# A transformer block with modulated LayerNorm: another order of normalising, transposing and modulating ahead of attention

## The chip, the cores and the metric

The kernel runs on one core of a Trainium2 chip (trn2). The metric is device time in microseconds (us); lower is better. The core has five engines with instruction streams of their own: TensorE (PE), VectorE (DVE), ScalarE (ACT), GpSimd (POOL) and SyncE (SP), which here issues all DMA transfers.

## The reference

The input has 2048 tokens of 1024 features; all tensors are bf16. There are 32 query heads of 32 features, one key head and one value head shared by all queries, and a feed-forward part with 3584 hidden features.

```python
mod = (silu(c) @ w_mod).reshape(1, 6, 1, -1)
sa, ca, ga, sb, cb, gb = mod[:, 0], ..., mod[:, 5]
h = layernorm(x) * (1 + ca) + sa
q, k, v = h @ wq, h @ wk, h @ wv           # q: 32 heads of 32; k, v: one head of 32
p = softmax(q k^T * 32 ** -0.5)            # for each head, over all 2048 keys
x = x + ga * ((p v) @ wo)
h = layernorm(x) * (1 + cb) + sb
x = x + gb * ((silu(h @ w1) * (h @ w3)) @ w2)
```

sa and ca come from the first 2048 columns of w_mod; the kernel calls the resulting vectors MODC 0 and MODC 1.

## The kernel before

**A planner orders the work.** The kernel is written as a list of nodes (`G.add`), each with its engine, a function that issues its instructions, an assumed duration (`dur`), what it reads and writes (keys), and a priority. `Dag.schedule` (L99) runs through an assumed time, takes for each engine the ready node that can start first, and among those the lowest priority number, then the earliest in the program. An instruction of VectorE with priority above 2 that has been ready for over 4 us moves up by 3. The result is a fixed order for each engine; `emit` (L256) writes it out with the semaphore waits. On the chip each engine follows its order strictly, whatever the real times are. Two prices matter below: one normalisation of a tile counts as 0.42 us on VectorE and 1.2 us on GpSimd (L525).

**PSUM banks.** There are eight banks: PB0, PB1 and the six of SP. A group of matmuls takes a bank with its first matmul and gives it back when it has been read out. Groups of one chain (`G.chain`) take their banks in program order. As long as `lend` is true, groups may also take banks of SP; once scores flow, those six belong to the scores, and all other work shares PB0 and PB1.

**Prologue (L427 to L713).** Tokens come in 16 tiles of 128. `ln_front(tb)` handles four tiles: mean and variance (two bn_stats of 512 columns and an aggregation on VectorE; for tiles 4 to 7 two passes on ScalarE, `ln_stats_act`, with small steps on GpSimd between), 1/sqrt for two tiles at a time on GpSimd (`ln_scale`), and the normalisation (`ln_norm`), for the last tile of every four but the first on GpSimd, otherwise on VectorE. X has eight slots, so the load of tile t + 8 waits for the normalisation of tile t. `ln_turn` transposes the normalised tiles on TensorE and copies them raw from PSUM into HREG, 1024 columns an instruction, on VectorE or ScalarE. This needs no modulation vector. The matmuls that make the vector (L628, 16 for each of eight 512 KB pieces of w_mod, the loads of L453) stand in a chain of their own. Once it is there (L634, L636), `ln_modulate` scales and shifts HREG in place, 8 instructions of 512 columns for each four tiles, on VectorE, ScalarE or GpSimd. Then come K projections (`kproj`), V projections (`vproj`) and the query projections (`qproj`) of the first 512 tokens, one for each group of four heads, f = 0 to 7. The loads of w_mod and wq are tied behind token loads with `after=`.

**Attention.** `attention(q0, qn, ...)` runs for five blocks of queries: two of 256 rows and three of 512. For each f it computes scores (L835), exponentials on ScalarE (L846, 1024 columns each; with 256 rows 16 of them for an f), products with V (L790), pairwise sums of the exponentials on VectorE (L875, L880) for the denominators, reciprocal (L900) and division (L902). Scores have the first priority on TensorE, value products come next, and all other matmuls are filler. An f needs all 16 key tiles, hence all four K projections.

**After attention.** `post(q0, qn)` holds the output projection (L920), the second LayerNorm, the transposes, and the feed-forward part (L943, ScalarE's tanh L952, VectorE L954 and L959, then L972). It is filler under the attention of the next blocks. HREG holds both the transposed tokens HT and the hidden features HHT, and WREG holds wq, pieces of w_mod and later the feed-forward weights; keys of 128 columns (`hk`) and 1024 columns (`wk`) say which part waits for which. The query projections of tokens 1024 to 2047 (`LATE`) are put off: `late_queries` (L682) comes after `post` of the second block, loads wq again (two transfers) and runs as filler in attention of the third block. `TS` and `TT` share their memory with `WKR`, the replicated key weights.

Of the kernel before, what the change touches and what calls it, by code (L numbers as in the profile page):

```python
# [8 lines left out]
P = 128  # L9
# [326 lines left out]
def build(nc, x_in, wq_in, wk_in, wv_in, wo_in, w1_in, w3_in, w2_in, c_in, wmod_in, out, S, D, F):  # L336
# [16 lines left out]
    LATE = (2, 3)  # L353
    LATE_AT = 1
# [17 lines left out]
    WKR_TS = sb("WKR", [P, NC * 128], BF16)  # L372
# [13 lines left out]

    HT = HREG[:].rearrange("p (b c s) -> p c b s", b=NTB, c=NC)
    TS = WKR_TS[:, 0:512]
    TT = WKR_TS[:, 512:1024]
    WKR = WKR_TS[:].rearrange("p (c a f) -> p c a f", c=NC, a=4)  # L390

    def hk(o, n):
        return [("H", i) for i in range(o // P, (o + n) // P)]

    def htk(c, tb):
        return hk((tb * NC + c) * 512, 512)

    def wk(a, n):
        return [("W", i) for i in range(a // 1024, (a + n) // 1024)]
# [46 lines left out]
    WQK = wk(0, NC * D)  # L446
# [4 lines left out]
    def wm01(k0, k1, after=()):  # L451
        for k in range(k0, k1):
            dma(lambda e, k=k: e.dma_start(WM01[:, k, :], wmod_in[k * P:(k + 1) * P, 0:2 * D]), ("wm01", k),  # L453
                writes=[("UR", k)], nbytes=P * 2 * D * 2, after=after)
# [57 lines left out]
    def xnt(q):  # L512

        return XN[:, q, :] if q < 4 else UREG[:, xnp[q // 2 - 2] * 2048 + q % 2 * D:][:, 0:D]

    def xnk(q):
        return [] if q < 4 else [("UR", xnp[q // 2 - 2])]

    xnp = [NU - 2, NU - 1, NU + NTR - 2, NU + NTR - 1]
# [7 lines left out]
    def ln_front(tb):  # L527

        if tb == 1:
            ln_stats_act(4, 4)  # L530
        else:
            for i in range(4):
                ln_stats(tb * 4 + i)
        for i in range(0, 4, 2):
            ln_scale(tb * 4 + i, 2)
        for i in range(4):
            ln_norm(tb * 4 + i, tb * 4 % 12 + i, "pool" if i == 3 and tb else "dve")
    ln_front(0)
    xl = xload(8, 4)
    ln_front(1)  # L540
    wm01(2, 5, xl)
    xl = xload(12, 4)
    wm01(5, NC, xl)
    dma(lambda e: e.dma_start(WQ[:, :, 0:P], wq_in[:, 0:P].rearrange("(c p) f -> p c f", p=P)), "wq0",
        writes=[("WQ", 0)] + WQK, nbytes=P * D * 2, after=xl)
# [4 lines left out]
    ln_front(2)  # L550

# [31 lines left out]
    def ln_turn(tb, q0, engs):  # L583

        for cb in range(NC // 2):
            g = grp()
            for i in range(4):
                def tr(e, i=i, g=g, cb=cb):
                    for h in range(2):
                        r = e.transpose(PBH[g.bank][:, h * 512 + i * P:h * 512 + (i + 1) * P],  # L590
                                        xnt(q0 + i)[:, (2 * cb + h) * P:(2 * cb + h + 1) * P], IDENT[:])
                    return r
                G.add("pe", tr, reads=[("XN", q0 + i), "IDENT"] + xnk(q0 + i), dur=0.13, lat=0.2,
                      acq=g if i == 0 else None, groups=[(g, "w")], mode="F")
            o = (tb * NC + 2 * cb) * 512
            if engs[cb % len(engs)] == "act":
                G.add("act", lambda e, g=g, o=o: e.activation(HREG[:, o:o + 1024], PBH[g.bank], ACT.Copy),
                      writes=hk(o, 1024), groups=[(g, "r")], dur=act_t(1024), prio=3)
            else:
                G.add("dve", lambda e, g=g, o=o: e.tensor_copy(HREG[:, o:o + 1024], PBH[g.bank]),  # L600
                      writes=hk(o, 1024), groups=[(g, "r")], dur=dve_t(1024, 2), prio=3)

    def ln_modulate(tb, engs):

        for c in range(NC):
            en = engs[c % len(engs)]
            if en == "act":
                G.add("act", lambda e, c=c: e.activation(HT[:, c, tb], HT[:, c, tb], ACT.Identity,
                                                         scale=MODC[:, 1, c:c + 1], bias=MODC[:, 0, c:c + 1]),
                      reads=htk(c, tb) + [("MODC", 0), ("MODC", 1)], writes=htk(c, tb), dur=act_t(512) + 0.04, prio=2)  # L610
            else:
                G.add(en, lambda e, c=c: e.tensor_scalar(HT[:, c, tb], HT[:, c, tb], MODC[:, 1, c:c + 1],
                                                         MODC[:, 0, c:c + 1], ALU.mult, ALU.add),
                      reads=htk(c, tb) + [("MODC", 0), ("MODC", 1)], writes=htk(c, tb),
                      dur=0.28 if en == "dve" else 0.75, prio=1)

    ln_turn(0, 0, ("dve", "act"))
    ln_turn(1, 4, ("act",))
    ln_front(3)
    ln_turn(2, 8, ("act", "dve"))  # L620
    ln_turn(3, 0, ("act", "dve"))

    G.chain = 3
    g = grp()
    for k in range(NC):
        def mm(e, k=k, g=g):
            for j in range(16):
                i = e.matmul(PB[g.bank][:, j:j + 1], WM01[:, k, j * P:(j + 1) * P], SCT[:, k:k + 1],  # L628
                             start=(k == 0 and j == 0), stop=True, skip_group_check=True)
            return i  # L630
        G.add("pe", mm, reads=["SCT", ("UR", k)], dur=16 * 0.06, lat=0.2, acq=g if k == 0 else None,
              groups=[(g, "w")], mode="F")
    G.chain = 0
    G.add("dve", lambda e, g=g: e.tensor_copy(MODC[:, 0, :], PB[g.bank][:, 0:8]), writes=[("MODC", 0)],  # L634
          groups=[(g, "r")], dur=0.13, prio=0)
    G.add("dve", lambda e, g=g: e.tensor_scalar(MODC[:, 1, :], PB[g.bank][:, 8:16], 1.0, None, ALU.add),  # L636
          writes=[("MODC", 1)], groups=[(g, "r")], dur=0.13, prio=0)
    G.add("pool", lambda e: e.tensor_copy(WKR, WKV[:, 0].unsqueeze(2).broadcast_to([P, NC, 4, 32])), reads=WKK,
          writes=["TS", "TT"], dur=1.3)

# [14 lines left out]
    def kproj(tb):  # L655
        sl = slice(tb * 512, (tb + 1) * 512)
        g = mm_group(NC, lambda e, b, c: e.matmul(b, WKR_TS[:, c * P:(c + 1) * P], HT[:, c, tb],
                                                  start=c == 0, stop=c == NC - 1),
                     lambda c: ["TS", "TT"] + htk(c, tb), late=0 if tb else NC - 1)
        G.add("dve", lambda e, g=g: e.tensor_copy(KT[:, sl], PB[g.bank]), writes=[("KT", tb)], groups=[(g, "r")],  # L660
              dur=dve_t(512), prio=1)

    def vproj(tb):
        def vmm(e, b, i):
            tt, c = i // NC, i % NC
            return e.matmul(b[:, tt * 32:(tt + 1) * 32], HT[:, c, tb, tt * P:(tt + 1) * P],
                            WKV[:, 1, c, :], start=c == 0, stop=c == NC - 1)
        g = mm_group(4 * NC, vmm, lambda i: WVK + htk(i % NC, tb), n_cols=72, per=NC)
# [4 lines left out]
    def qproj(tb, f, w=None, wkeys=None):  # L673
        sl = slice(tb * 512, (tb + 1) * 512)
        w = WQ[:, :, f * P:(f + 1) * P] if w is None else w
        wkeys = WQK + [("WQ", min(f, 1))] if wkeys is None else wkeys
        g = mm_group(NC, lambda e, b, c: e.matmul(b, w[:, c, :], HT[:, c, tb], start=c == 0, stop=c == NC - 1),  # L677
                     lambda c: wkeys + htk(c, tb), late=0 if tb or f else NC - 1)
        G.add("dve", lambda e, g=g: e.tensor_copy(QT[:, f, sl], PB[g.bank]),
              writes=qkeys(f, tb * 512, 512), groups=[(g, "r")], dur=dve_t(512), prio=1)  # L680

    def late_queries(tbs):  # L682

        G.chain = 2
        for a in range(2):
            o = a * NF * 256
            w = WR[:, o:o + NC * 512].rearrange("p (c f) -> p c f", c=NC)
            dma(lambda e, a=a, w=w: e.dma_start(w, wq_in[:, a * 512:(a + 1) * 512].rearrange("(c p) f -> p c f", p=P)),
                ("w2", a), writes=wk(o, NC * 512), nbytes=NC * P * 1024)
            for i in range(4):  # L690
                for tb in tbs:
                    qproj(tb, a * 4 + i, w[:, :, i * P:(i + 1) * P], wk(o, NC * 512))
# [4 lines left out]
    ln_modulate(0, ("dve", "act"))  # L697
    kproj(0)
    qproj(0, 0)
    lend[0] = False  # L700
    ln_modulate(1, ("act", "dve"))
    kproj(1)
    vproj(0)
    ln_modulate(2, ("dve", "pool"))
    kproj(2)
    vproj(1)
    ln_modulate(3, ("pool", "dve"))
    kproj(3)
    vproj(2)
    vproj(3)  # L710
# [4 lines left out]
    def wms(i):  # L715
        return wk(NC * D + i * 2048, 2048)
# [54 lines left out]
    for tb in range(1, NTB):  # L771
        for f in range(NC):
            if tb not in LATE:
                qproj(tb, f)
# [133 lines left out]
    def post(q0, qn):  # L908
        t0, nt = q0 // P, qn // P
        npk = 512 // qn  # L910
        HHT = HREG[:, 0:NF * qn].rearrange("p (f s) -> p f s", f=NF)
        o2 = NF * qn if qn == 256 else NF * 512
        O2B = HREG[:, o2:o2 + 1024].rearrange("p (a t d) -> p a t d", a=2, t=2)
# [17 lines left out]
        for ft in range(NF):  # L931
            sl, sub = (ft // 2) % 2, ft % 2
            if sub == 0:
                c0 = ft * P
                for w, src in enumerate((w1_in, w3_in)):
                    dma(lambda e, c0=c0, sl=sl, w=w, src=src: e.dma_start(
                        W13[sl][w], src[:, c0:c0 + 256].rearrange("(c p) f -> p c f", p=P)),
                        ("w13", w, sl), writes=wk(sl * NF * 256 + w * 2048, 2048), nbytes=D * 512)
# [6 lines left out]
            wks = [wk(sl * NF * 256 + w * 2048, 2048) for w in range(2)]  # L945
# [104 lines left out]
```

The softmax here doesn't subtract the row's maximum and nothing guards it: scores larger than these inputs give would overflow.

## Time and profile before

| What | Value |
|---|---|
| Runs | 1309.62, 1309.38 and 1307.08 us, median 1309.38 |
| Profiled execution: its own time, and its span | 1309.62 us, 1307.5 us |
| TensorE, ScalarE, VectorE, GpSimd busy | 1180.5, 1029.8, 875.5, 43.2 us |
| Mean granted TensorE clock | 0.962 |
| First and last exponential start | 53.6 and 1098.9 us |
| Exponentials | 1024, 970.4 us busy |
| Modulation vector (L634, L636) | 43.8 to 44.0 us |

Times within the span start at its first instruction; the profiled execution's own time is 2.1 us longer than its span. In the profile, L12 is line 12 of the kernel. "PEld" is TensorE's loading of weights, which overlaps its matmuls. In the table by slices each digit is the busy share of one of 40 equal slices in tenths (9 is 90% or more), and PEclk is the granted TensorE clock in tenths of full speed. In the tables by stretch, a row gives the stretch, its length, then the busy time and number of instructions of each engine, the granted clock, the DMA share and GB/s. In a list of waits, "A <- B: total, times, longest" means that A stood idle until B released it. In the chain of waits a row is start, duration and what ran. For one line, the three durations are minimum, median and maximum in ns, followed by the first and last start in us.

### The profile page before, as it was taken

How to read it: one execution, taken by the hardware profiler on the slowest of the kernel's cores; microseconds unless marked ns; L12 is line 12 of the kernel's file. 1: busy time of each engine (PE TensorE's matmuls, PEld its weight loads, DVE VectorE, ACT ScalarE, POOL GpSimd, SP SyncE). 2: the span in 40 equal slices, each digit the busy share in tenths (PEclk: the TensorE clock that was granted, in tenths of full speed). 3: DMA queues.
4: the chain of work that ended last, by engine and by line, in shares of the span. 5: the costliest groups of instructions: out<-in, count | busy, mean ns of one | idle time of the engine just before them, and what ended most of it. 6: DMA issues, size and time to landing. Idle time of an engine off the chain costs nothing.

```text
span 1307.5 us, 26890 instructions
## 1 busy us (share of the span) xinstructions
PE 1180.5 (90%) x11424; PEld 594.5 (45%) x11513; DVE 875.5 (67%) x1206; ACT 1029.8 (79%) x1200; POOL 43.2 (3%) x73
## 2 busy tenths in 40 slices
PE   5788778889898889988899999999999999999998
PEld 4443324554454555323333335545333336764477
DVE  6688857886457778856588777655887777633321
ACT  5699989999889999989899999988999996011100
POOL 5300000000000000000000000000000000000000
PEclk7897968999899999999999999999999999999999
DMA  7625101554356566220133224402422344255563
GB/s 262 242 69 159 50 2 48 142 136 122 87 132 178 147 170 174 91 65 1 34 97 97 84 79 114 114 1 66 130 85 87 88 122 114 57 164 159 157 174 89
DMA packets 241528, 143.43 MB, mean 110 GB/s; under 512 B 6912, under 2 KB 233216, under 8 KB 241408
## 3 DMA queue, kind: packets, MB, share of 16 engines
q1 hardware_dynamic: 241408, 141.71, 38.1%
q8 instruction: 91, 1.49, 0.5%
q14 instruction: 29, 0.24, 0.1%
HBM read 137.50 MB, written 4.19 MB: 108 GB/s over the span
## 4 chain that ended last, share of the span: by engine, by line
ACT 43%; PE 41%; issue 7%; DVE 5%; DMA 1%; POOL 0%; SPq 0%; ACTq 0%; DVEq 0%
ACT UREG L846 40%; PE PB L943 9%; PE PB L972 7%; PE SP L835 5%; PE SP L943 5%; PE PB L790 5%; PE SP L972 5%; ACT WKR L952 3%; PE PB L920 2%; DVE UREG L875 1%; PE PB L891 1%; PE SP L920 1%; PE PB L677 1%; DVE UREG L880 1%; DMA WREG<-in_B_w_dram 1%
## 5 line engine op out<-in xcount | busy, mean ns | idle before, releaser
L846 ACT ACTIVATE UREG<-SP 128x1024 bf16<-128x1024 f32 x1024 | 970.4, 1181 | 59.1 <-PE PB L790 40.2
L943 PE MATMUL PB<-QT,WREG 128*128 128x512 bf16 (+1 forms) x1861 | 358.1, 331 | 22.2 <-issue 6.0
L880 DVE TENSOR_TENSOR UREG<-UREG 128x2048 bf16<-128x2048 bf16 x200 | 243.7, 1219 | 29.6 <-ACT UREG L846 26.8
L835 PE MATMUL SP<-QT,KT 32*128 32x512 bf16 (+1 forms) x2560 | 208.7, 351 | 51.7 <-ACT UREG L846 40.2
L943 PEld LDWEIGHTS PB<-QT,WREG 128*128 128x128 bf16 x1904 | 166.5, 98 | 174.4 <-issue 73.7
L875 DVE TENSOR_TENSOR UREG<-UREG 128x2048 bf16<-128x2048 bf16 x100 | 121.5, 1215 | 90.8 <-ACT UREG L846 90.7
L835 PEld LDWEIGHTS SP<-QT,KT 32*128 32x128 bf16 x2560 | 54.3, 92 | 239.1 <-ACT UREG L846 231.0
L972 PE MATMUL PB<-WREG,HREG 128*128 128x256 bf16 x1232 | 153.0, 273 | 0.0
L790 PE MATMUL PB<-UREG,V 128*32 128x512 bf16 (+1 forms) x2528 | 139.7, 356 | 10.4 <-DVE WKR L954 4.7
L972 PEld LDWEIGHTS PB<-WREG,HREG 128*128 128x128 bf16 x1232 | 113.2, 98 | 37.8 <-issue 24.2
L952 ACT ACTIVATE WKR<-PB 128x512 bf16<-128x512 f32 (+1 forms) x126 | 85.1, 676 | 44.5 <-PE PB L943 41.6
L900 DVE RECIPROCAL DSB<-DSB 128x128 f32<-128x128 f32 x128 | 114.7, 926 | 0.7
L954 DVE SCALAR_TENSOR_TENSOR WKR<-WKR,PB 128x512 bf16<-128x512 bf16 (+1 forms) x126 | 70.7, 561 | 44.8 <-ACT WKR L952 40.6
L790 PEld LDWEIGHTS PB<-UREG,V 128*32 128x32 bf16 x2528 | 60.1, 100 | 72.9 <-issue 24.4
L952 ACT ACTIVATE WKR<-SP 128x512 bf16<-128x512 f32 x14 | 8.4, 597 | 94.5 <-PE SP L943 94.5
L943 PE MATMUL SP<-QT,WREG 128*128 128x512 bf16 x330 | 74.5, 379 | 0.3
L972 PE MATMUL SP<-WREG,HREG 128*128 128x256 bf16 x560 | 62.8, 273 | 1.4 <-DMA WREG<-in_B_w_dram 1.4
L959 DVE TENSOR_TENSOR HREG<-WKR,PB 128x256 bf16<-128x256 bf16 (+1 forms) x112 | 60.5, 540 | 4.6 <-PE PB L943 3.2
L677 PE MATMUL PB<-HREG,WREG 128*128 128x512 bf16 x233 | 58.3, 381 | 2.4 <-issue 1.4
L972 PEld LDWEIGHTS SP<-WREG,HREG 128*128 128x128 bf16 x560 | 54.7, 98 | 8.9 <-DMA WREG<-in_B_w_dram 1.9
L920 PE MATMUL PB<-WO,QT 128*128 128x512 bf16 x192 | 52.2, 396 | 2.6 <-issue 1.0
L943 PEld LDWEIGHTS SP<-QT,WREG 128*128 128x128 bf16 x336 | 32.9, 98 | 39.4
(106 smaller groups left out, 626.9 us busy)
## 6 DMA issues: line engine op xcount, KB each, us to landing
WREG<-in_B_w_dram SPq DMA_DIRECT2D x140, 512.0 KB, 4.1
WREG<-in_B_w_dram SPq DMA_DIRECT2D x20, 1792.0 KB, 8.2
X<-in_A_x_dram SPq DMA_DIRECT2D x32, 256.0 KB, 3.8
WREG<-in_w_mod_dram SPq DMA_DIRECT2D x16, 512.0 KB, 5.1
UREG<-in_w_mod_dram SPq DMA_DIRECT2D x8, 512.0 KB, 6.2
out_dram<-X SPq DMA_DIRECT2D x16, 256.0 KB, 3.1
WO<-in_A_wo_dram SPq DMA_DIRECT2D x1, 2048.0 KB, 16.8
WREG<-in_A_wq_dram SPq DMA_DIRECT2D x2, 1024.0 KB, 5.1
```

The costliest lines, as they stand in the source:

```text
L677: g = mm_group(NC, lambda e, b, c: e.matmul(b, w[:, c, :], HT[:, c, tb], start=c == 0, stop=c == NC - 1), lambda c: wkeys + htk(c, tb), la ...
L790: r = e.matmul(PB[g.bank][32 * gg:32 * gg + 32, 0:qn], V[:, kt, :] if kind == "V" else ONES[:], U[:, pu, (gg * npk + j) * qn:(gg * npk + j ...
L835: r = e.matmul(SP[:, b, o:o + w], KT[32 * gg:32 * gg + 32, kts[j] * P:(kts[j] + 1) * P], QT[32 * gg:32 * gg + 32, f, q0 + qo:q0 + qo + w], ...
L846: G.add("act", lambda e, u=u, h0=h0, n=n, b0=b0, nb=nb, wb=wb: e.activation(U[:, u, h0 * W:(h0 + n) * W].rearrange("p (b w) -> p b w", b=n ...
L875: G.add("dve", lambda e, tr=tr, u=u, fu=first_u: e.tensor_tensor(TR[:, tr, 0:4 * W], U[:, fu, 0:4 * W], U[:, u, 0:4 * W], ALU.add), reads= ...
L880: G.add("dve", lambda e, tr=tr, u=u: e.tensor_tensor(TR[:, tr, 0:4 * W], TR[:, tr, 0:4 * W], U[:, u, 0:4 * W], ALU.add), reads=[("TR", tr) ...
L900: G.add("dve", lambda e, h=h: e.reciprocal(DSB[:, h * 128:(h + 1) * 128], DSB[:, h * 128:(h + 1) * 128]), reads=["DSB"], writes=[("DSBr", ...
L920: g = mm_group(NC, lambda e, b, f, t=t, h=h: e.matmul(b, QT[:, f, t * P:(t + 1) * P], WO[:, f, h * 512:(h + 1) * 512], start=f == 0, stop= ...
L943: return e.matmul(b[:, o:o + qn], W13[sl][w][:, c, sub * P:(sub + 1) * P], QT[:, c, q0:q0 + qn], start=c == 0, stop=c == NC - 1)
L952: G.add("act", lambda e, g=g1: e.activation(TS[:, 0:qn], PB[g.bank][:, 0:qn], ACT.Tanh, scale=0.5), writes=["TS"], groups=[(g1, "r")], dur ...
L954: G.add("dve", lambda e, g=g1: e.scalar_tensor_tensor(TT[:, 0:qn], TS[:, 0:qn], 1.0, PB[g.bank][:, 0:qn], ALU.add, ALU.mult), reads=["TS"] ...
L972: return e.matmul(b[:, j * 256:(j + 1) * 256], HHT[:, fc, (i0 + j) * P:(i0 + j + 1) * P], W2S[:, r, fc, :], start=fc == 0, stop=fc == NF - 1)
```

## The change

Raw copies and modulation in place go; the transposed tile is modulated as it leaves PSUM (`ln_transpose`, which the second LayerNorm uses already): for the first eight tiles every other bank by ScalarE, all others by VectorE. The matmuls of the modulation vector stand in the main chain ahead of all transposes. The transposes of tiles 8 to 15 come after the first K, Q and V projections, when only PB0 and PB1 are free to them. The loads of w_mod pieces 2 to 7 and of the first part of wq no longer wait for tokens. The scale of four tiles is computed at once, and the last tile of every four, now also tile 3, is normalised on GpSimd. `LATE` goes: the queries of all tokens are projected in the main chain, behind the gates. HT is laid out by feature chunk, TS and TT move into HREG and WKR gets memory of its own. The fine keys become coarse: the first write of each user of HREG after the prologue waits for all readers of HT, and the first feed-forward weight loads wait for all readers of wq and of the w_mod pieces.

```diff
-    LATE = (2, 3)
-    LATE_AT = 1
...
-    WKR_TS = sb("WKR", [P, NC * 128], BF16)
+    WKR = sb("WKR", [P, NC, 4, 32], BF16)
...
-    HT = HREG[:].rearrange("p (b c s) -> p c b s", b=NTB, c=NC)
+    HT = HREG[:].rearrange("p (c s) -> p c s", c=NC)
+    HHT = HREG[:, 0:NF * 512].rearrange("p (f s) -> p f s", f=NF)
+    o = NF * 512
+    TS = HREG[:, o:o + 512]
+    TT = HREG[:, o + 512:o + 1024]
+    O2B = HREG[:, o + 1024:o + 2048].rearrange("p (a t d) -> p a t d", a=2, t=2)
+    HKEY = "HREG"
...
-        return XN[:, q, :] if q < 4 else UREG[:, xnp[q // 2 - 2] * 2048 + q % 2 * D:][:, 0:D]
+        return XN[:, q, :] if q < 4 else UREG[:, (NU + NTR - 1) * 2048 - (q - 4) // 2 * 2048 + q % 2 * D:][:, 0:D]
...
-        for i in range(0, 4, 2):
-            ln_scale(tb * 4 + i, 2)
+        ln_scale(tb * 4, 4)
         for i in range(4):
-            ln_norm(tb * 4 + i, tb * 4 % 12 + i, "pool" if i == 3 and tb else "dve")
+            ln_norm(tb * 4 + i, tb * 4 % 12 + i, "pool" if i == 3 else "dve")
     ln_front(0)
-    xl = xload(8, 4)
+    xload(8, 4)
+    wm01(2, NC)
+    dma(lambda e: e.dma_start(WQ[:, :, 0:P], wq_in[:, 0:P].rearrange("(c p) f -> p c f", p=P)), "wq0",
+        writes=[("WQ", 0)] + WQK, nbytes=P * D * 2)
     ln_front(1)
-    wm01(2, 5, xl)
     xl = xload(12, 4)
-    wm01(5, NC, xl)
-    dma(lambda e: e.dma_start(WQ[:, :, 0:P], wq_in[:, 0:P].rearrange("(c p) f -> p c f", p=P)), "wq0",
-        writes=[("WQ", 0)] + WQK, nbytes=P * D * 2, after=xl)
...
     ln_front(2)
+
+    g = grp()
+    for k in range(NC):
+        def mm(e, k=k, g=g):
+            for j in range(16):
+                i = e.matmul(PB[g.bank][:, j:j + 1], WM01[:, k, j * P:(j + 1) * P], SCT[:, k:k + 1],
+                             start=(k == 0 and j == 0), stop=True, skip_group_check=True)
+            return i
...
-    ln_turn(0, 0, ("dve", "act"))
-    ln_turn(1, 4, ("act",))
-    ln_front(3)
-    ln_turn(2, 8, ("act", "dve"))
-    ln_turn(3, 0, ("act", "dve"))
-
-    G.chain = 3
...
-    ln_modulate(0, ("dve", "act"))
-    kproj(0)
-    qproj(0, 0)
-    lend[0] = False
-    ln_modulate(1, ("act", "dve"))
-    kproj(1)
-    vproj(0)
-    ln_modulate(2, ("dve", "pool"))
-    kproj(2)
-    vproj(1)
-    ln_modulate(3, ("pool", "dve"))
-    kproj(3)
-    vproj(2)
-    vproj(3)
+    for tb in range(NTB):
+        if tb == 3:
+            ln_front(3)
+        ln_transpose(4, tb * 4 % 12, lambda c, tb=tb: HT[:, c, tb * 512:(tb + 1) * 512],
+                     lambda c, tb=tb: [("HT", c, tb)], 0, 1, ("act", "dve") if tb < 2 else ("dve",))
+        if tb == 1:
+            kproj(0)
+            qproj(0, 0)
+            lend[0] = False
+            kproj(1)
+            vproj(0)
+            vproj(1)
+        elif tb:
+            kproj(tb)
+            vproj(tb)
     for f in range(1, NC):
         qproj(0, f)
...
     for tb in range(1, NTB):
         for f in range(NC):
-            if tb not in LATE:
-                qproj(tb, f)
+            qproj(tb, f)
...
             G.add("act", lambda e, g=g1: e.activation(TS[:, 0:qn], PB[g.bank][:, 0:qn], ACT.Tanh, scale=0.5),
-                  writes=["TS"], groups=[(g1, "r")], dur=act_t(qn), prio=-1)
+                  writes=["TS"] + alias("TS"), groups=[(g1, "r")], dur=act_t(qn), prio=-1)
...
+    def wa(kind, sl):
+
+        if (kind, sl) in first_wa:
+            return []
+        first_wa.add((kind, sl))
+        return [("WMS", i) for i in range(3)] + WQK + [("WQ", 0), ("WQ", 1)]
...
         post(q0, qn)
-        if bi == LATE_AT:
-            late_queries(LATE)
```

## The prediction

> **What bounds the kernel now.** I read the busy table by slices first, then sums over stretches that I cut where the work changes, then the chain of waits, then single groups.
>
> ```profile
> PE   5788778889898889988899999999999999999998
> ACT  5699989999889999989899999988999996011100
> PEclk7897968999899999999999999999999999999999
> ```
>
> ScalarE is full from the second slice until the last exponential, TensorE in the tail. The sums over stretches (length, then busy time of TensorE, its loads, VectorE, ScalarE, GpSimd; granted clock; DMA):
>
> ```profile
> 30.00:53.60 23.60, 14.94 (x155) 9.97 (x155) 15.40 (x31) 12.26 (x16) 14.57 (x14) 0.68 1.05 361
> 53.60:71.20 17.60, 15.68 (x261) 8.29 (x267) 12.02 (x18) 14.86 (x16) 0.00 (x0) 1.00 0.04 15
> 71.20:155.00 83.80, 71.10 (x1052) 31.46 (x1060) 71.68 (x95) 81.24 (x88) 0.00 (x0) 0.87 0.37 108
> 155.00:188.00 33.00, 19.97 (x297) 8.04 (x295) 19.24 (x24) 30.04 (x33) 0.00 (x0) 0.60 0.01 3
> 310.00:587.00 277.00, 252.63 (x2415) 132.62 (x2421) 188.38 (x258) 256.83 (x302) 1.58 (x4) 0.98 0.47 130
> 587.00:1099.00 512.00, 480.86 (x3992) 195.41 (x4039) 375.23 (x462) 482.48 (x552) 6.31 (x16) 1.00 0.28 80
> ```
>
> The first exponential (L846) starts at 53.58 and the first head group (16 of them) is done at 71.2. From there to 587 (attention of blocks 0 to 2) ScalarE is 92 to 98% busy: it sets the pace. From 587 to 1099 TensorE holds it up:
>
> ```profile
> ACT UREG L846 <- PE PB L790: 28.7, 14, 4.9
> ```
>
> After 1099 only TensorE works (202 of 208 us). So the time is the start of steady exponentials, plus ScalarE's work to 587, plus 720 us whose work the change leaves alone. The chain shows what starts the first stage:
>
> ```profile
> 37.54 4.08 POOL XN L523
> 43.17 0.69 DVE HREG L600
> 43.86 0.07 DVE MODC L634
> 44.04 7.13 DVE HREG L612 x11
> 53.07 0.43 PE SP L835 x8
> ```
>
> GpSimd normalises tile 15; its transposes and raw copies end as the modulation vector arrives at 44.0; VectorE modulates; scores follow.
>
> **What the Trainium skill says.** "GPSIMD Engine Reference", section 3.1, gives 1.8 to 2.6 cycles an element at 1.2 GHz: for 1024 elements an estimate of 1.5 to 2.2 us. The trace has about twice that, and that decides:
>
> ```profile
> L523 POOL TENSOR_SCALAR UREG<-X,MV,RS x2: 3781/3786/3792, 24.2 to 28.0; 128x1024 bf16<-128x1024 bf16 x2
> L523 DVE TENSOR_SCALAR XN<-X,MV,RS x23: 493/545/548, 10.8 to 1131.7; 128x1024 bf16<-128x1024 bf16 x23
> L577 DVE TENSOR_SCALAR QT<-PB,MODC x34: 396/532/544, 205.8 to 1135.0; 128x512 bf16<-128x512 bf16 x18, 128x256 bf16<-128x256 bf16 x16
> L480 DVE BATCH_NORM_STATS2 ST<-X x24: 639/675/695, 5.7 to 34.0; 128x6 f32<-128x512 bf16 x24
> ```
>
> "DMA: Bandwidth & Descriptors", section Queues, rings and completion order: one queue's descriptors are consumed in ring order, so a load issued behind others comes after them. The trace agrees: loads into L453's tiles land 3.8 to 7.9 us after issue, with queued bytes ahead of them. "TensorE: Matmul & The Clock Gate", What's actually happening: an idle window halves the clock. The trace agrees: 0.60 granted from 155 to 188, when no filler was left, and a score step of eight matmuls takes 0.61 us there, 0.40 us elsewhere.
>
> **The change part by part.**
>
> (1) Loads. The six loads wm 2 to 7 and wq0 no longer wait for tokens, so they are issued back to back by about 10.5 us (0.43 us each). Ahead of wm7's end lie 6.4 MB; the trace moves near 400 GB/s when fed, so it lands near 21.5 us. Now it is issued at 29.0, and its matmuls run at 42.9, behind the transposes of tile 15 in TensorE's order. On SP the loads of tiles 8 to 11 are moved behind all this, and land near 23 to 26; now they are there before 20. Tile 11's load waits for tile 3's slot until 16.4 (part 2), which costs nothing while the queue is full.
>
> (2) Modulation vector. Tile 3 moves to GpSimd: 4.0 us for 0.5. The row means of tiles 4 to 7 (L492) queue behind it on GpSimd: from 13.5 to 16.4. ScalarE's four squares (1.15 each) end at 21.5 (20.5 now, with a raw copy between); scale of four, about 2 us; GpSimd normalises tile 7 from 23.5 to 27.5. The planner prices that step 1.2 us, so it should put tile 7's transposes ahead of the last vector matmuls in TensorE's strict order: they wait with it. Then 0.6 us of transposes, 48 matmuls at 0.03 to 0.035, so the vector is ready near 30.4, against 44.0: 13.6 earlier.
>
> (3) Copies. Gone: 10 raw copies on ScalarE (1.02), 6 on VectorE (0.69), and the modulations in place, 8 on ScalarE (0.80), 16 on VectorE (0.56), 8 on GpSimd (0.79). New: 8 evacuations with scale on ScalarE and 24 on VectorE (0.532, L577). ScalarE's form isn't in the trace: between 0.68 (the tanh of this size from PSUM, L952) and 0.80 (L608); I take 0.75, so 6 us. The sum on VectorE is the same within 0.3 us, but **all of it now comes after the vector**, with the statistics of tiles 8 to 15 behind it in VectorE's order, because the planner's own prices (loads one after another at 300 GB/s, L240) put the vector at about 24.8 of its assumed time and tile 8 at 25.2; so close a call can fall the other way.
>
> (4) The ramp. ScalarE's evacuations end near 37 and the first exponential starts near 38, 15 us earlier. But only eight can run on the keys of tiles 0 to 7. VectorE owes, from the vector on until tile 15's statistics: evacuations of tiles 0 to 7, where ScalarE takes every other bank, 8, and of tiles 8 to 11 all 8, together 16 x 0.53 = 8.5; statistics 8 x 1.25 = 10; three norms 1.6; K, Q, V copies 4 x 0.68 + 2 x 0.28 = 3.3; three or four pairwise adds at 1.2 = 4; vector copies and ASB 0.7: 28. With 1 us of gaps this is 59.4. Behind it in series: scale 1.4, GpSimd's tile 15 at 4.1, transposes 0.6, eight evacuations in two pairs of banks 4.8, K projection 2.0, its copy 0.7, Q projection of the second head group (it takes its bank after K3 and V3) 2.2, its copy 0.7: 16.5, and 2 us for adds that grew old and go first: 78, where now it is 71.2. Exponentials 9 to 16 stall meanwhile. Cost **+6.7 us**. If statistics get ahead of the vector and adds stay out, 67 (-4); if each GpSimd norm holds up TensorE's order as well, 84 (+13).
>
> (5) Queries of tiles 8 to 15. The 16 groups (128 matmuls of 512 columns, 28 us) move from the stretch up to 579 to behind L771's first eight. Eight groups took 34 us from 121 on (4.2 each), so 24 end near 220, beside attention that ScalarE bounds. The stretch 155 to 188 gets filler and full clock: its six pauses of about 0.75 us before L846 fall away, -4.5; filler takes banks from value batches, as from 65 to 155, +1.5. At 550 to 587 the reverse: no filler, slow clock, up to four such pauses (+3), but the stall of 4.6 at 556 has no queries beside it; I take +1.5. Sum **-1.5**. The first feed-forward, at 212 now, starts near 220 (its weights wait for the last query, about 5 us to land); the 28 us freed at 550 cover this. If not, that is the third rival.
>
> (6) The coarser keys, other layout of HT, TS and TT in HREG: no added instruction. The first weight load of the feed-forward (L936) now waits on SP for the last query and gate; behind it on SP stand only its sisters, as the tokens for the first two blocks are loaded at 44 to 48. The first tanh and the first write of HHT wait for every reader of HT; behind the tanh on ScalarE are exponentials, but its own matmuls need that same weight load, so the wait is over when it comes: 0, and if TensorE's order put another query behind it, one pause of some 4 us. Tiles 4 to 11 normalised lie in other slots of UREG, free before the first pair sum that uses them: 0. The two reloads of wq (1 MB each) go; they ran under DMA at about half load with no wait for them on ScalarE: 0.
>
> Sum: +6.7 - 1.5 = +5.2 on the profiled execution's 1309.6 (span 1307.5 and 2.1 around it; median of the runs 1309.4): 1314.8, **1315**.
>
> **Rivals.** First, faster: the vector's 13.6 us arrive. It needs VectorE to finish tiles 8 to 15 early, by statistics done in its idle time before 30 us. For it: VectorE was busy only 19.6 of the 29.5 us from 14.3 to 43.8. Steady exponentials at 67, -4.2, and -3 for the filled stretch: 1302. It decides if the second head group starts before 70. Second, no change: the ramp costs 3 and the fuller stretch gives 3: 1310. For it: ScalarE needs 15 us for the first 16 exponentials either way. Third, much slower: 28 us of queries early delay both 256-row feed-forwards so that the second isn't done when block 2's attention ends; what is late runs in the stretch that TensorE bounds, at full price. Against it: the second feed-forward's last matmul (L972) is done by 550, with 37 us to spare. Half of the 28 us back, and the ramp: 1328.
>
> **How the numbers follow.** A difference under 0.2% (2.6 us) can't be told from none here. My case 0.50, within it 1308 to 1322; faster 0.20; no change 0.15; much slower 0.15. Of my case four fifths end over 1312.2, the rest within; the rivals go to their sides: faster 0.20, same 0.25, slower 0.55. Low end 1302, the first rival's time; high end 1330, just over the third's. The likeliest case alone: 1308 to 1322.
>
> **What would show it.** MODC's copies near 30 (not 25, not 40); first L846 near 38; a hole of several us after the eighth L846, ended by VectorE or tile 11's norm on GpSimd; the 17th L846 near 78; granted clock near 1 from 155 to 188; block 2's attention over near 592. It is wrong if the hole is missing, if VectorE idles in the ramp, or if 592 is met and the end isn't 720 later.

## The result and the profile after

The changed kernel takes **1315.37 us** (median of four runs, 1314.11 to 1316.20) against 1309.35 for the kernel before in the same session: a ratio of 1.0049, with a 95% interval of 1.0032 to 1.0066. It is about 6 us slower; 1315.0 was predicted. The profiled execution took 1314.11 (span 1312.3) against 1309.62 (span 1307.5), so the two traces differ by 4.8 us.

The busy table by slices of the kernel after, with the lines shown before:

```profile
PE   5688998899899888958899999999999999999998
ACT  3459999999899999989999999989999996011100
PEclk7777999999899999969999999999999999999999
```

ScalarE fills up one slice later (3 4 5 9 instead of 5 6 9 9), and the clock stays at 7 for four slices. Nothing is gained at the start. The hole in the clock at about 160 to 190 us is gone; another stands in the slice from 558 to 590, where the prediction expected one. The sums over the same stretches up to 587 (length; busy time of TensorE, its loads, VectorE, ScalarE, GpSimd; clock; DMA):

```profile
30.00:53.60 23.60, 15.76 (x210) 9.46 (x208) 16.95 (x38) 12.89 (x16) 6.32 (x3) 0.72 0.82 281
53.60:71.20 17.60, 8.77 (x95) 5.35 (x95) 13.28 (x26) 3.77 (x4) 6.50 (x3) 0.69 0.16 57
71.20:155.00 83.80, 72.44 (x1002) 32.81 (x1012) 67.90 (x91) 72.05 (x78) 0.00 (x0) 0.87 0.28 86
155.00:188.00 33.00, 30.54 (x382) 12.72 (x388) 29.08 (x38) 32.92 (x37) 0.00 (x0) 1.00 0.01 2
310.00:587.00 277.00, 238.41 (x2431) 129.58 (x2432) 185.77 (x257) 258.66 (x307) 1.58 (x4) 0.95 0.49 134
```

From 53.6 to 71.2 ScalarE works 3.77 us where it worked 14.86. From 155 to 188 it works 32.92 where it worked 30.04, at full clock. ScalarE's part of the timeline (start, length, operation, and in brackets the idle time before it and what ended it) shows the whole start:

```profile
39.22 7.44 ACT L778 ACTIVATE UREG<-SP 128x1024 bf16<-128x1024 f32 x8 [2.37 <-PE SP L767]
62.49 3.77 ACT L778 ACTIVATE UREG<-SP 128x1024 bf16<-128x1024 f32 x4 [15.84 <-PE SP L767]
79.61 3.97 ACT L778 ACTIVATE UREG<-SP 128x1024 bf16<-128x1024 f32 x4 [13.34 <-PE SP L767]
```

Eight exponentials start at 39.22, over 14 us earlier than before. Then ScalarE waits 15.8 us for the keys of tiles 8 to 11 and 13.3 us for those of tiles 12 to 15. The list of waits for the first 90 us puts a sum on it (waiting engine and line, releaser, total, times, longest); before, the row of the exponentials had 6.6 us there:

```profile
ACT UREG L778 <- PE SP L767: 32.1, 4, 15.8
```

In the chain of the kernel after, followed back from 86 us, the last hole reads:

```profile
64.75 4.37 POOL XN L512
...
69.60 1.90 DVE HREG L580 x4
71.50 1.13 DVE UREG L807
72.63 1.82 DVE HREG L580 x4
...
74.90 3.19 PE PB L602 x7
```

GpSimd normalises tile 15, VectorE evacuates eight banks with a pair sum between, TensorE projects the keys at 0.46 us a matmul.

Because each kernel has 1,024 exponentials of one size, the start of the n-th one in each trace is a clock for the whole program. The table is worked out from these starts (us); the last column is what each stretch added to the difference.

| exponential | before | after | after − before | added since the row above |
|---|---|---|---|---|
| 1st | 53.58 | 39.22 | −14.4 | −14.4 |
| 9th | 60.82 | 62.49 | +1.7 | +16.0 |
| 17th | 71.22 | 84.17 | +12.95 | +11.3 |
| 112th | 161.65 | 174.76 | +13.1 | +0.15 |
| 160th | 209.82 | 218.77 | +8.95 | −4.15 |
| 192nd | 242.47 | 249.43 | +6.95 | −2.0 |
| 500th | 554.98 | 563.16 | +8.2 | +1.2 |
| 512th | 570.78 | 575.24 | +4.5 | −3.7 |
| 1024th | 1098.94 | 1103.87 | +4.9 | +0.5 |

The tail after the last start is 208.6 us before and 208.4 after. So the start costs **13 us**, and **8 us** come back after it, by steps that lie between the 112th and the 512th exponential (−8.65 there, +0.65 elsewhere). The prediction had 6.7 and 1.5.

### The profile page after: what moved, and what is told of

It is laid out like the page before. It is cut to its first block, busy times and chain, and to the rows that moved or that the text cites. A ratio compares the mean times of both kernels' runs of the same rounds, so it can differ in the third digit from the quotient of the medians.

```text
span 1312.3 us, 26854 instructions
## 1 busy us (share of the span) xinstructions
PE 1178.0 (90%) x11422; PEld 595.0 (45%) x11513; DVE 872.2 (66%) x1207; ACT 1019.8 (78%) x1190; POOL 40.0 (3%) x58
## 4 chain that ended last, share of the span: by engine, by line
ACT 41%; PE 40%; issue 6%; DVE 5%; DMA 2%; POOL 0%; ACTq 0%; SPq 0%; DVEq 0%
ACT UREG L778 38%; PE PB L872 9%; PE PB L901 7%; PE SP L872 5%; PE SP L767 5%; PE SP L901 5%; PE PB L722 5%; ACT HREG L881 3%; PE PB L849 2%; DVE UREG L807 1%; DMA WREG<-in_B_w_dram 1%; PE PB L823 1%; PE SP L849 1%; DMA WREG<-in_w_mod_dram 1%; DVE UREG L812 1%
## 5 line engine op out<-in xcount | busy, mean ns | idle before, releaser
L872 PE MATMUL PB<-QT,WREG 128*128 128x512 bf16 (+1 forms) x1861 | 354.5, 330 | 10.7 <-issue 4.2
L767 PE MATMUL SP<-QT,KT 32*128 32x512 bf16 (+1 forms) x2560 | 208.4, 350 | 54.0 <-ACT UREG L778 45.9
L881 ACT ACTIVATE HREG<-PB 128x512 bf16<-128x512 f32 (+1 forms) x126 | 83.1, 660 | 46.4 <-PE PB L872 42.2
L883 DVE SCALAR_TENSOR_TENSOR HREG<-HREG,PB 128x512 bf16<-128x512 bf16 (+1 forms) x126 | 70.9, 563 | 45.9 <-ACT HREG L881 37.7
L881 ACT ACTIVATE HREG<-SP 128x512 bf16<-128x512 f32 x14 | 8.4, 597 | 94.5 <-PE SP L872 94.5
L888 DVE TENSOR_TENSOR HREG<-HREG,PB 128x256 bf16<-128x256 bf16 (+1 forms) x112 | 60.8, 543 | 5.4 <-PE PB L872 3.9
```

The lines of the kernel that those rows point to most:

```text
L767: r = e.matmul(SP[:, b, o:o + w], KT[32 * gg:32 * gg + 32, kts[j] * P:(kts[j] + 1) * P], QT[32 * gg:32 * gg + 32, f, q0 + qo:q0 + qo + w], ...
L872: return e.matmul(b[:, o:o + qn], W13[sl][w][:, c, sub * P:(sub + 1) * P], QT[:, c, q0:q0 + qn], start=c == 0, stop=c == NC - 1)
L881: G.add("act", lambda e, g=g1: e.activation(TS[:, 0:qn], PB[g.bank][:, 0:qn], ACT.Tanh, scale=0.5), writes=["TS"] + alias("TS"), groups=[( ...
L883: G.add("dve", lambda e, g=g1: e.scalar_tensor_tensor(TT[:, 0:qn], TS[:, 0:qn], 1.0, PB[g.bank][:, 0:qn], ALU.add, ALU.mult), reads=["TS"] ...
L888: G.add("dve", lambda e, g=g3, ft=ft, o3=o3: e.tensor_tensor(HHT[:, ft, 0:qn], TT[:, 0:qn], PB[g.bank][:, o3:o3 + qn], ALU.mult), reads=[" ...
```

## The experiments

The explanation to be tested was: normalisations of 4 us on GpSimd, put there by a planner that prices them at 1.2, together with VectorE's work that now stands behind the vector, make the hole; early queries act as filler for TensorE and give part back. The rivals were: the hole comes of the score banks, kept free too early; the give-back is only work moved out of a later stretch; the clock doesn't matter. Each measured time is a median, and the ratio is to runs of the kernel before on the same chip (medians 1308.91 for e1 to e4, 1309.61 for e5 to e8, 1307.88 for e9 to e12). "17th" is the start of the 17th exponential; "112 to 160" and "500 to 512" are the times between those exponentials (before: 48.17 and 15.80; after: 44.01 and 12.09). The traces of e1, e2, e5 and e12 are of executions 2.4 to 3.6 us above the medians, so stretches read from them need not add up to the median's difference.

**The change cut in two: the queries alone.** The kernel before, with no late queries:

```diff
-    LATE = (2, 3)
+    LATE = ()
...
-        if bi == LATE_AT:
+        if LATE and bi == LATE_AT:
```

> The kernel before, with its own prologue and keys, but all query projections early, as in the changed kernel (LATE empty). My theory: the changed kernel's early queries give back about 8 us of the 13 us that its ramp loses, since they fill TensorE from 150 to 212 (full clock, no pauses between head groups) and no longer stand beside the value products at 556. Then the 17th exponential stays at 71 us and the end comes at 1301.5 (1299 to 1304). Rival: what is given back belongs to the ramp itself, because work piles up done while ScalarE stands idle there; then this edit alone gives nothing, 1309 (1307 to 1311), or costs some us by contention for the two free banks.

Measured 1305.86 us, ratio 0.9971 [0.9961, 0.9981]: faster, but less than expected and outside the range of 1299 to 1304. Both stretches answered: 112 to 160 took 44.14, 500 to 512 took 12.30, together −7.5 us. Some 5 us were lost again between the 160th and the 192nd in the profiled execution (1309.48, the slowest of nine). SyncE's part of its timeline, and ScalarE's waits from 200 to 250:

```profile
227.32 28.93 SPq L936 DMA_DIRECT2D WREG<-in_B_w_dram  x9
```

```profile
ACT UREG L846 <- PE SP L835: 4.6, 4, 2.5
ACT UREG L846 <- PE PB L790: 2.6, 1, 2.6
```

The first feed-forward's weights are issued only when the last query is done, and TensorE's order has feed-forward matmuls ahead of scores. A pause of this size is what part 6 of the prediction allowed for, but for another reason: there it hung on the coarser keys, which this kernel doesn't have. In the kernel after ScalarE lost 0.5 us at that place.

**The change cut in two: the prologue alone.** The kernel before with the new prologue (load order, tile 3 on GpSimd, scales of four tiles at once, the vector ahead of the transposes, these evacuated with scale); late queries and fine keys stay. The core of the edit:

```diff
-        for i in range(0, 4, 2):
-            ln_scale(tb * 4 + i, 2)
+        ln_scale(tb * 4, 4)
...
-    ln_modulate(0, ("dve", "act"))
-    kproj(0)
...
+    for tb in range(NTB):
+        if tb == 3:
+            ln_front(3)
+        ln_transpose(4, tb * 4 % 12, lambda c, tb=tb: HT[:, c, tb],
+                     lambda c, tb=tb: htk(c, tb), 0, 1, ("act", "dve") if tb < 2 else ("dve",))
```

> The kernel before with the changed kernel's prologue alone (load order, tile 3 on GpSimd, vector first, modulation on the way out of PSUM); queries of tiles 8 to 15 stay late and the fine keys stay. My theory, that ramp and queries add up: 17th exponential near 84, pauses again between 155 and 188 at a clock near 0.6, end at 1322 (1319 to 1325). Rival, that the ramp gives part of its loss back by itself: 1315 (1313 to 1317).

Measured 1321.39, 1.0096 [1.0081, 1.0111], as expected. 17th at 85.62, 112 to 160 took 49.15, 500 to 512 15.79: the start is lost, and on balance nothing comes back by the 512th. From 155 to 188:

```profile
155.00:188.00 33.00, 20.30 (x317) 8.54 (x314) 24.56 (x31) 30.76 (x34) 0.00 (x0) 0.72 0.18 49
```

TensorE is busy 20 of 33 us again, at a clock of 0.72. So the prologue costs 12.5 us, and the queries (with the coarser keys) that after has and this kernel lacks are worth about 6. The halves don't add exactly: in the old prologue the queries alone (e1) were worth 3.

**The GpSimd normalisations taken away.** The kernel after, with every normalisation on VectorE:

```diff
-            ln_norm(tb * 4 + i, tb * 4 % 12 + i, "pool" if i == 3 else "dve")
+            ln_norm(tb * 4 + i, tb * 4 % 12 + i, "dve")
```

> The changed kernel with the last tile of every four normalised on VectorE instead of GpSimd. If GpSimd's four normalisations (3.9 to 5.1 us each, each in series with the transposes behind it) carry the ramp: vector near 24 instead of 31, each of the two holes about 4 us shorter, 17th exponential near 70 instead of 84, end 1301 (1298 to 1305). If VectorE's own work after the vector carries it: the vector comes 7 us earlier and nothing else is won, 17th exponential 77, end 1308. If it is the two free banks and the order of the two batches of tiles: 17th exponential at 80 or later, end over 1311.

Measured 1304.44, 0.9963 [0.9950, 0.9975]. Four more instructions on VectorE, and the kernel is 11 us faster than after, within the range for the case that GpSimd's steps carry the ramp, though the 17th exponential was expected near 70. The vector is there at 25.9, the first exponential at 33.9, the 17th at 73.58.

**The same edit on the kernel before.**

```diff
-            ln_norm(tb * 4 + i, tb * 4 % 12 + i, "pool" if i == 3 and tb else "dve")
+            ln_norm(tb * 4 + i, tb * 4 % 12 + i, "dve")
```

> The kernel before with the three GpSimd normalisations (tiles 7, 11, 15) on VectorE. If GpSimd's step is as costly in this prologue too, where the chain runs through tile 15's: vector near 39 instead of 44, 17th exponential near 67, end 1305 (1302 to 1307). If the last pieces of w_mod or VectorE's load set the vector's time: 17th exponential at 70 or later, 1308 or more.

Measured 1300.51, 0.9935 [0.9920, 0.9950], more than expected. The kernel before gains as well: the vector comes at 37.0, the 17th exponential at 62.87. This run matters most for attribution. Against it, e3 is still 10.7 us late at the 17th. The GpSimd steps cost the kernel after 10.6 us at that point and the kernel before 8.4: they make the kernel after slow, but only some 2 of the 13 us by which its start is later than before.

**Only the price corrected.** The kernel after; the normalisations stay on GpSimd, and the planner is told what they take:

```diff
-              reads=..., writes=..., dur=0.42 if en == "dve" else 1.2, prio=2)
+              reads=..., writes=..., dur=0.42 if en == "dve" else 4.0, prio=2)
```

> The changed kernel; only the planner's price for a normalisation on GpSimd is set from 1.2 to 4.0 us. No instruction is added, removed or moved to another engine, only the order changes: VectorE takes the statistics of tiles 12 to 15 ahead of the evacuations that wait for tile 11. If strict order behind a step that the planner holds for short is a large part of the ramp: 17th exponential near 74 instead of 84, end 1305 (1302 to 1308). If the duration of GpSimd's step itself is what counts, wherever it stands: 17th exponential 82 to 85, end 1313 to 1316.

Measured 1303.71, 0.9960 [0.9946, 0.9973]: 11.7 us better than after, from the order alone: the two programs have the same number of instructions on every engine. 17th at 74.01. Timeline of VectorE around the normalisation of tile 11, first of after, then of this kernel:

```profile
49.09 0.20 DVE L473 BATCH_NORM_AGGREGATE MV<-ST 128x2 f32<-128x12 f32 x1
52.96 1.90 DVE L580 TENSOR_SCALAR HREG<-PB,MODC 128x512 bf16<-128x512 bf16 x4 [3.67 <-PE PB L565]
54.78 0.68 DVE L471 BATCH_NORM_STATS2 ST<-X 128x6 f32<-128x512 bf16 x1
```

```profile
46.24 1.20 DVE L807 TENSOR_TENSOR UREG<-UREG 128x2048 bf16<-128x2048 bf16 x1
...
47.48 1.82 DVE L471 BATCH_NORM_STATS2 ST<-X 128x6 f32<-128x512 bf16 x3
49.42 1.90 DVE L580 TENSOR_SCALAR HREG<-PB,MODC 128x512 bf16<-128x512 bf16 x4
```

In after, VectorE stands 3.67 us in front of an evacuation whose input isn't there, with statistics of tiles 13 to 15 queued behind it, ready to run. With the right price they go ahead, and the wait is gone. The vector comes earlier too (27.5 instead of 31.1), since TensorE's order no longer has its last matmuls behind tile 7's transposes. In both kernels the tile-11 step itself is on GpSimd (47.21 to 52.26 in after, 44.81 to 48.72 here).

**The same price in the kernel before.** The same edit of 1.2 to 4.0:

> The kernel before with the planner's price for a normalisation on GpSimd set from 1.2 to 4.0 us, nothing else. If a wrong price in front of a strict order costs in this prologue too: the last matmuls of the vector go ahead of tile 15's transposes, the vector comes near 38 instead of 44, 17th exponential near 67, end 1305 (1302 to 1307). If GpSimd's step is on the path whatever the order: 17th exponential 70 to 72, 1308 to 1311.

Measured 1302.83, 0.9958 [0.9942, 0.9973], 17th at 64.23. So the wrong price cost the kernel before as well. With the right one in both, the changed kernel (0.9960) and the kernel before (0.9958) can't be told apart; with the normalisations on VectorE in both, the change costs 0.28%, 3.7 us.

**Half the GpSimd steps.** The kernel after, with tiles 11 and 15 alone on VectorE, so that the vector stays late:

```diff
-            ln_norm(tb * 4 + i, tb * 4 % 12 + i, "pool" if i == 3 else "dve")
+            ln_norm(tb * 4 + i, tb * 4 % 12 + i, "pool" if i == 3 and tb < 2 else "dve")
```

> The changed kernel with only tiles 11 and 15 normalised on VectorE; tiles 3 and 7 stay on GpSimd, so the vector stays near 31 and the first exponential at 39. Third run: -5.3 us by an earlier vector, and -5.3 in the two holes. If these two parts add up: 17th exponential near 79 instead of 84, end 1310 (1308 to 1312). If the holes alone carry the ramp and the vector's time is of no weight: 17th exponential 74 to 75, end 1305. If only the vector counts: 84 and 1315.

Measured 1310.87, 1.0018 [1.0011, 1.0026], 17th at 79.52 with the vector at 31.9. The two late steps are worth 4.7 us at the 17th exponential. The step from here to e3, which has the two early ones gone too, is another 5.9, close to the 5.2 us by which e3's vector is earlier than after's: both parts count.

**The score banks.** e3 with the banks of the scores lent to the prologue until all keys and values are projected:

```diff
-            lend[0] = False
...
         elif tb:
             kproj(tb)
             vproj(tb)
+    lend[0] = False
```

> The changed kernel with all normalisations on VectorE (as in the third run) and, added, the six score banks open to the transposes and projections of tiles 8 to 15 whenever no scores hold them. If two free banks for the transposes make the holes that were left (9th exponential at 55.1, 13th at 69.2, 17th at 73.6): 13th near 63, 17th near 68, end 1300 (1297 to 1302). If VectorE's order and work make them: within 1.5 us of the third run, 1304.

Measured 1306.01, 0.9979 [0.9970, 0.9989]; 17th at 74.01 against 73.58 in e3. No gain. But the run decides less than was meant: in its trace all 64 transposes of tiles 8 to 15 still go to PB0 and PB1, and only one V projection takes a score bank. What speaks against the rival is how long the transposes wait for a bank to be read out. TensorE's waits of after, from 46 to 75:

```profile
PE PB L565 <- DVE HREG L580: 0.9, 2, 0.7
```

That is 0.9 us (1.5 in e3), beside holes of 15.8 and 13.3 us.

**Filler that does nothing.** The kernel before, with 96 added matmuls of 512 columns whose results go unused; their planned place is the attention of block 0:

```diff
+    for _ in range(12):
+        g = grp()
+        for i in range(8):
+            G.add("pe", lambda e, g=g: e.matmul(PB[g.bank], IDENT[:], HT[:, 0, 0], start=True, stop=True),
+                  reads=["IDENT"] + htk(0, 0), dur=MM, lat=0.2, acq=g if i == 0 else None, groups=[(g, "w")], mode="F")
```

> The kernel before with 96 added matmuls of 512 columns whose results are not used, in twelve groups behind the last early query projection, so that TensorE has filler from about 150 on; queries of tiles 8 to 15 stay late. It adds work and moves none. If the gain at 155 to 188 is the clock alone: granted clock near 1 there, the pauses before the exponentials gone, 129th exponential some 4 us earlier than 179.0, end 1305 (1303 to 1307). If it is the work moved out of the stretch to 579 that counts: 1309 to 1312, since the added matmuls only take banks.

Measured 1301.44, 0.9940 [0.9928, 0.9953]: 7.5 us faster with work added. From 155 to 188:

```profile
155.00:188.00 33.00, 32.44 (x392) 12.86 (x391) 21.41 (x26) 33.00 (x37) 0.00 (x0) 1.00 0.06 15
```

Clock 1.00, ScalarE without a gap, and 112 to 160 took 43.96, the same as with early queries. That is the first part of the give-back without anything moved. That the clock is how the filler does it is read from the two traces (0.60 before, 1.00 here) and isn't shown apart from the filler. The run also gained 5.4 us from 160 to 512, more than expected, and lost 2.3 after. The planner's later order differs, which may be why; that part isn't explained. Among the kernels here the time from 160 to 512 lies between 355.6 and 365.0 without a single cause.

**The clock alone.** The kernel before, with eight such matmuls, unknown to the planner, ahead of the first value product and of the denominator in four head groups of block 0:

```diff
+                for _ in range(warm if w0 == 0 else 0):
+                    e.matmul(PB[g.bank], IDENT[:], KT[:, 0:512], start=True, stop=True)
...
```

> The kernel before with eight dummy matmuls of 512 columns ahead of the first value product and of the denominator sum in the last four head groups of block 0, in the bank that these overwrite anyway: 96 in all, priced at nothing, so that every engine's order of the real work is the same as before. If the clock is what early filler gives: granted clock over 0.9 from 155 to 188, 129th exponential about 4 us earlier (175), and as ScalarE sets the pace up to 587, the end 4 us earlier, 1305 (1303 to 1307). If the gain of the fourth run came from another order of the later work: 1308 to 1311.

Measured 1332.72, 1.0176 [1.0147, 1.0205]: a miss. The blocks stand in front of scores in TensorE's order, and ScalarE's waits from 120 to 200 read

```profile
ACT UREG L848 <- PE SP L837: 17.9, 10, 3.4
```

so the clock was not isolated (it rose to 0.85 from 155 to 188, and 112 to 160 took 56.82). The run shows something else: it was 20.2 us late at the 160th exponential and 22.5 at the end. In this kernel a delay in block 0 goes through to the end in full.

**Both remedies in the kernel before.** e8 with tiles 8 to 11 taken out of the late queries, and e8 with e4's 96 unused matmuls:

```diff
-    LATE = (2, 3)
+    LATE = (3,)
```

> The kernel before with its normalisations on VectorE (eighth run) and the queries of tiles 8 to 11 early, those of tiles 12 to 15 late. Eight groups should fill the stretch of the last head groups of block 0 (exponentials 112 to 160 in 44 us instead of 48.4) and yet be done before the first feed-forward weights are needed. If the two gains add up: 4.2 below the eighth run, 1296 (1294 to 1299). If they do not, because an earlier start leaves the same filler to run out earlier: 1300.

> The kernel before with its normalisations on VectorE (eighth run) and the 96 dummy matmuls of the fourth run, results unused. If filler is worth the same on top: exponentials 112 to 160 in 44 us, end 1296 (1293 to 1299), like the run with half of the queries early, although here no work is moved. If moved work counts beyond filler, this run ends later than that one by 2 us or more.

e11: 1295.02, 0.9900 [0.9885, 0.9915]; e12: **1292.57**, 0.9874 [0.9857, 0.9892], the fastest kernel here by its median. Half the queries as filler give a third of the first gain (112 to 160 took 46.77, in e8 48.34) and over half of the second (500 to 512 took 13.87, in e8 15.79), and matmuls that do nothing give all of the first (43.83) and none of the second (15.84). The intervals of the two overlap; what is shown is that the first gain needs no moved work, not which of the two is faster.

## Why the prediction was right

The time was met to 0.4 us, but that is luck: two errors of 6.3 and 6.5 us cancel in it. The direction rests on mechanisms that the runs support.

**Vector (parts 1 and 2): right.** 31.1 measured, 30.4 predicted, by the path named: tile 3 on GpSimd from 12.43 to 16.8, the row means behind it at 16.87, tile 7 from 24.82, its transposes ahead of the last vector matmuls in TensorE's order:

```profile
24.82 3.91 POOL L512 TENSOR_SCALAR UREG<-X,MV,RS 128x1024 bf16<-128x1024 bf16 x1 [1.30 <-DVE UREG L512]
28.79 0.61 PE L565 MATMUL SP<-IDENT,UREG 128*128 128x128 bf16 x4 [1.80 <-POOL UREG L512]
30.04 1.04 PE L543 MATMUL SP<-SCT,UREG 128*128 128x1 bf16 x32
31.12 0.17 DVE L548 COPY MODC<-SP 128x8 f32<-128x8 f32 x1 [6.05 <-PE SP L543]
```

**Copies (part 3): right.** 0.534 us on VectorE; ScalarE's form took 0.77 to 0.81 where 0.75 was taken. The open question of order fell as taken: the statistics of tiles 8 to 15 run after the vector.

**The ramp (part 4): mechanism right, size off.** First exponential 39.2 (38 predicted), the hole after the eighth, with tile 11's normalisation on GpSimd in its path. The 17th came at 84.17 instead of 78, near the upper bound named (84). The three terms of that sum, in the kernels with this prologue (e3, e5: the runs above):

| us | predicted | after | e3 | e5 |
|---|---|---|---|---|
| vector | 30.4 | 31.1 | 25.9 | 27.5 |
| until the statistics of tile 15 are done | 29.0 | 31.2 | 28.7 | 27.4 |
| from there to the 17th exponential | 18.5 | 21.9 | 19.0 | 19.1 |
| 17th | 78 | 84.2 | 73.6 | 74.0 |

The second term was 28 of work and 1 of gaps. VectorE's busy time in that stretch of after is 25.4, so the work was a little less and the gaps nearly 6; 3.67 of them are the one wait shown above. An idle VectorE in the ramp was one of the prediction's own signs of being wrong, and it came in part. In e3 it is 25.6 busy of 28.7: there VectorE's debt is nearly the whole term, as the prediction had it. The third term is the one that was most mis-sized. The scale of four took 2.2 (1.4 taken), tile 15's normalisation 4.36 (4.1), the K projection 3.2 to 3.6 (2.0), the query projections behind it 4.4 (2.2). The K projection ran at half clock: 0.50 was granted from 74.9 to 78.1, while e5's ran at 1.00 and the same seven matmuls took half as long. "TensorE: Matmul & The Clock Gate", What's actually happening, puts the slow clock after an idle window of about 3.4 us. The trace agrees only in part: TensorE was busy 3.95 of the 9.9 us before the K projection of after and 7.35 of 9.66 before that of e5, but in after it was never idle there for more than 2.4 us at a time. The query projections lost little to the clock (0.81 granted, then 1.00): TensorE's order has two of them there, 15 recorded matmuls, where the sum had one, and at full clock e3 takes 4.1 for them too. The two PE lines, of after and of e5:

```profile
74.90 3.19 PE L602 MATMUL PB<-HREG,WKR 128*128 128x512 bf16 x7 [2.31 <-DVE HREG L580]
```

```profile
66.66 1.67 PE L602 MATMUL PB<-HREG,WKR 128*128 128x512 bf16 x7 [1.42 <-DVE HREG L580]
```

So of the 12.95 us that the ramp costs against the kernel before, 10 to 11 remain when both kernels have their normalisations on VectorE (73.58 against 62.87) or both the right price (74.01 against 64.23): by the traces that is work which stood ahead of the vector and now stands behind it, and the serial end that follows; no run moves this work back, so it isn't shown by experiment. Two to three are the change's own share of the GpSimd steps: it adds one, and its holes and late vector meet a strict order made for 1.2 us.

**The queries (part 5): direction right, size off.** −1.5 predicted, −8.0 found from the 17th exponential to the last. The six pauses were put at −4.5 and the stretch from 112 to 160 gave −4.15. The contention of +1.5 that was set against it did not show. The stretch from 550 on was put at +1.5, four pauses against one stall; the pauses came (ScalarE waits 5.1 us for scores from 550 to 592), but all save 1.1 of that fell behind the 512th exponential, in the stretch that TensorE bounds, where after is only 0.5 us longer. What counted is the stall of before, which is gone and gave 3.7:

```profile
560.83 4.69 ACT L846 ACTIVATE UREG<-SP 128x1024 bf16<-128x1024 f32 x5 [4.55 <-PE PB L790]
```

The stall does belong to late queries: it is there in all kernels that keep them (15.8), half of it with half of them (13.9, e11), and gone in those that have none (12.1 to 12.3). The small rest of the −8.0 (−2.0 from 160 to 192, +1.2 to 500, +0.65 elsewhere) stays open.

**The fixed rest: right.** From the 513th exponential to the 1024th all kernels take 526.5 to 529.5, and the tail after it didn't move, so what is late at the 512th is late at the end.

**The rivals.** "Faster" gave as its point of decision a second head group before 70; that was not met in after, nor in e3 (73.6), which was faster than before by another way: its give-back. "Much slower" by late feed-forwards did not happen, though they came later than predicted: the first one's weights were issued at 231.5 and its matmuls started at 240.4 (near 220 predicted, 212 before). The last matmul of the second starts at 555.0 (531.0 before), ahead of the last exponential of block 2, so the freed time covered it.

## What to carry to other kernels

Where a planner fixes each engine's order, measure what a step takes on the engine it is put on: one price of 1.2 for a step of 4 us cost 12 us in one kernel and 5 to 6 in the other, with the same instructions on every engine. Starting the bottleneck's engine earlier is worth only as much as the inputs of its next work are early too: ask what the ninth instruction waits for, not only the first. Before a change is credited or blamed for a cost, make the same edit in the kernel before: of the 10.6 us that GpSimd's steps cost this ramp, 8.4 were in the old one too.

## What was not expected of the hardware

- The same normalisation of 128x1024 took 3.78 to 5.05 us on GpSimd. VectorE's took 0.54 alone and up to 1.43 beside a GpSimd one. "SBUF — State Buffer", SBUF: two separate sides, says that the two engines share a port pair that one holds for a whole instruction. The tile-11 step of after (5.05) has a pair sum of VectorE beside it; but in e5 the step took 3.91 with a pair sum beside it, which took its usual 1.20. So the traces show that the two slow each other at times, and not a rule for when.
- 96 matmuls whose results nobody reads made a kernel 7.5 us faster (e4), and a kernel already improved about 8 us faster (e8 to e12, 0.9935 to 0.9874): TensorE ran at 1.00 instead of 0.60 to 0.67 from 155 to 188, and ScalarE, which sets the pace there, had no gaps left.
- In the kernel before the clock fell to 0.60 in a stretch (155 to 188) where TensorE was busy 20 of 33 us and never idle for more than 1.44 us at a time. The prediction took this as agreeing with the idle window that it cites; the trace shows the slow clock without an idle stretch of 3.4 us.
